# Transposing a layer norm's output by DMA, as 16-bit halves, instead of on TensorE

## The chip, the cores and the metric

The kernel runs on one core of one Trainium2 chip. The metric is the device time of one execution in microseconds (us); lower is better. The names of the engines are those of the profile: PE (TensorE, matrix products; PEld are its weight loads), DVE (VectorE), ACT (ScalarE), POOL (GpSimd), SP (SyncE, which here issues nearly all DMAs; its queue is written SPq).

## The reference

All data is 32-bit float. 2048 tokens of width 512 pass through a linear-attention half and a gated half, each behind a layer norm that is modulated by a scale and a shift; six vectors of width 512 come from a small product of `c`.

```python
mod = (_silu(c) @ w_mod).reshape(c.shape[0], 6, 1, -1)
sa, ca, ga, sb, cb, gb = (mod[:, 0], mod[:, 1], mod[:, 2], mod[:, 3], mod[:, 4], mod[:, 5])
h = _layernorm(x, axis=-1) * (1 + ca) + sa
x = x + ga * _A_ref(h, A_wqkv, A_wo)          # linear attention, 32 heads of 16
h = _layernorm(x, axis=-1) * (1 + cb) + sb    # the second layer norm
x = x + gb * _B_ref(h, B_w_gate, B_w_up, B_w_down)   # ((h Wg) * (h Wu)) Wd, Wg and Wu are 512 x 1376
```

## The kernel before, in words

**Tiles.** The 2048 tokens are 4 chunks (0 to 3) of 4 token tiles of 128. Every product is done in three matmuls on operands split into a high and a low part (`split`: ACT makes the high part, DVE or POOL the low one).

**The second layer norm** of a chunk has these steps. `xhat` (L277, ACT) makes four normalized tiles `n[j]` of 128 tokens x 512. `transpose` (L284, PE) turns them into four tiles of 128 features x 512 tokens, 16 transposes of 128x128 a chunk, into banks of PSUM. `ln2_f` (L925, ACT) applies scale `cb` and shift `sb` to each of the four and writes `f`. For chunks 2 and 3, `f` goes to memory (`kept`, L930) and is loaded back later (L111, by `Left.get`).

**The gated half** works in two sides: chunks 0 and 1, then chunks 2 and 3. A side is 11 blocks, one for each 128 columns of the two weights, so block n runs from 0 to 21. A block multiplies by a Strassen-like scheme with 7 products: `times` into the four PSUM banks a, b, c, d (`abank` to `dbank`), 6 matmuls each (L1057), in the order a11, s1, s2, a12, s3, a22, s4. Between them stand copies of one bank into another on ACT (L1063, `copy`): b from a after a11, c from b after s2; then u2, g, and u3. DVE reads the banks with L1113 (which frees d), L1122 and L1083. A bank's next product waits for the copy into it. Part s2 of a block therefore waits for the copy into b, and part s3 for the copy into c.

**What stands between.** `block` calls `also(point)` after each part: at the points a11, s1, s2, a12, s3, pe, mid and s4, lists of jobs written by hand are run. `early` holds the jobs of the attention half's end and of the second layer norm of chunks 2 and 3. The point pe, between s3 and a22, holds other matmuls (`y_a`, L871, and the down products, L1146 to L1148); their results are added to `x` by DVE (L1153) at s4 in the first side. `split_down` and `scale_down` (L1280, then ACT and DVE L206 and L207) prepare down weights; `right_load`, `right_sums`, `right_split` and `right_keep` load, sum (POOL L1002), split (ACT L1013 and L1016, POOL L1020) and store (SP L1034) the weights of blocks ahead.

Each engine runs its instructions in the order in which the program issues them, and an instruction that waits holds up all behind it on its engine. SP's queue does the same with DMAs: an issue that waits holds up later issues. Each DMA of SP has one of eight semaphores in turn, and waits until the DMA eight issues earlier has landed. Tiles in SBUF come from one pool of 99 buffers; a new tile waits for the last reader of the tile that had the buffer before.

Of the kernel before, what the change touches and what calls it, by code (L numbers as in the profile page):

```python
# [7 lines left out]

F32 = mybir.dt.float32
F32R = mybir.dt.float32r  # L10
AF = mybir.ActivationFunctionType
ALU = mybir.AluOpType
AX = mybir.AxisListType

P = 128
# [7 lines left out]
def tile_adaln_block(  # L23
# [12 lines left out]
    nc = tc.nc  # L36
    ctx.enter_context(tc.manual_schedule())
    _, S, D = x.shape
    F = w_gate.shape[1]
    KD = D // P  # L40
    NJ = 4
    CH = NJ * P
# [22 lines left out]
    def f32(ap):  # L65
        return ap.bitcast(F32)
# [3 lines left out]
    def T(p, tag, shape=(P, D), dt=F32, bufs=None):  # L70
        cnt[0] += 1
        return p.tile(list(shape), dt, tag="t" if p is tiles else tag, name=f"{tag}_{cnt[0]}", bufs=bufs)

    def B(tag, shape=(P, D), dt=F32):

        return T(tiles, tag, shape, dt)
# [11 lines left out]
    nc.gpsimd.memset(ones, 1.0)  # L88
    ones_r = consts.tile([P, P], F32R, name="ones_r")
    mask = consts.tile([P, P], F32, name="mask")  # L90
# [53 lines left out]

    idle = B("w", dt=F32R)
    idle_f = B("f")
# [15 lines left out]
    def silu_a():  # L162
        nc.tensor.transpose(ct, c_k, ident[:KD, :KD])
        nc.scalar.activation(ce, ct, AF.Exp, scale=-1.0)

# [6 lines left out]
    def mod_acc(acc, raws, ks, on=None):  # L172
        for k in ks:
            if k == 0:
                if on:
                    on.activation(acc, raws[k], AF.Copy, scale=sc[:, 0:1])
                else:
# [19 lines left out]
    def mod_row(v, pair):  # L197
        ps = bank()
        over_rows(ps, pair)
        t = consts.tile([P, D], F32, name=f"row{v}")  # L200
        nc.scalar.activation(t, ps, AF.Copy)
        return t


    def split(src, h, l, low=None):
        nc.scalar.activation(h, src, AF.Copy)  # L206
        (low or nc.vector).tensor_tensor(l, src, f32(h), op=ALU.subtract)  # L207

    def split_raw(raw, shape=(P, D), low=None):
        h = B("w", shape, F32R)  # L210
        l = B("w", shape, F32R)
        split(raw, h[:raw.shape[0]], l[:raw.shape[0]], low)
        return h, l
# [25 lines left out]
    class Norm:  # L239
        def __init__(self, tiles):  # L240
            self.tiles = tiles
            self.mv = T(small, "mv", (P, NJ, 2), bufs=6)
            self.n = [None] * NJ
            self.ps = [None] * KD
            self.t = [None] * KD

        def stats(self, *js, of=None):
            for j in js:
                st = T(small, "st", (P, 6), bufs=4)
                nc.vector.bn_stats(st, self.tiles[j] if of is None else of)  # L250
                nc.vector.bn_aggr(self.mv[:, j], st)
# [18 lines left out]
        def xhat(self, *js, on=None):  # L270
            for j in js:
                self.n[j] = B("n")
                if on:
                    on.tensor_scalar(self.n[j], self.tiles[j], self.rstd[:, j:j + 1], self.nmr[:, j:j + 1],
                                     op0=ALU.mult, op1=ALU.add)
                    continue
                nc.scalar.activation(self.n[j], self.tiles[j], AF.Identity,  # L277
                                     scale=self.rstd[:, j:j + 1], bias=self.nmr[:, j:j + 1])

        def transpose(self, *ks, of=bank):  # L280
            for k in ks:
                ps = of()
                for j in range(NJ):
                    nc.tensor.transpose(ps[:, j * P:(j + 1) * P], self.n[j][:, k * P:(k + 1) * P], ident)  # L284
                self.ps[k] = ps

        def banks(self):

            a, b, c, d = [bank() for _ in range(KD)]
            self.ps = [(a[:, :2 * P], ps_idle[:, 2 * P:]), (b,), (c,), (d,)]  # L290
# [6 lines left out]
        def modulated(self, scale, shift, *ks, keep=None, cast=None):  # L297
            for k in ks:
                h = B("h", dt=F32R)
                l = B("h", dt=F32R)  # L300
                f = B("f")
                nc.scalar.activation(f, self.ps[k], AF.Identity, scale=scale[:, k:k + 1], bias=shift[:, k:k + 1])
                if cast:
# [119 lines left out]
    halves = {}  # L423
# [222 lines left out]
    for i in range(4, NT):  # L646
        ch, j = divmod(i, NJ)
# [194 lines left out]
    def turn_a(i, of=bank):  # L842
        tps[i] = of()
        phi = phq.pop(i)
        for k in range(KD):
            nc.tensor.transpose(tps[i][:, k * P:(k + 1) * P], phi[:, k * P:(k + 1) * P], ident)

    def turn_h(i):
        pqs[i] = (B("xh", dt=F32R), B("xl", dt=F32R))
        nc.scalar.activation(pqs[i][0], tps[i], AF.Copy)  # L850

    def turn_l(i):
        h, l = pqs[i]
        nc.vector.tensor_tensor(l, tps.pop(i), f32(h), op=ALU.subtract)
# [8 lines left out]
    def y_a(i):  # L863
        pq = pqs.pop(i)
        fresh = i not in seeded
        if fresh:
            yps[i] = acc_bank()
        for k in range(KD):
            (ah, al), (bh, bl) = cut(pq, k * P, (k + 1) * P), wp[k]
            for n, (x, y) in enumerate(((ah, bh), (ah, bl), (al, bh))):  # L870
                nc.tensor.matmul(yps[i], x, y, start=fresh and k + n == 0,  # L871
                                 stop=k == KD - 1 and n == 2, skip_group_check=True)

    def y_b(i):
        ch, j = divmod(i, NJ)
        ps = yps.pop(i)
        if i in seeded:
            nc.scalar.activation(xts[ch][j], ps, AF.Copy)
            norm2[ch].stats(j, of=ps)
        else:  # L880
            nc.vector.tensor_tensor(xts[ch][j], xts[ch][j], ps, op=ALU.add)
            norm2[ch].stats(j)
# [30 lines left out]
    norm2 = {ch: Norm(xts[ch]) for ch in range(NCH)}  # L913
# [5 lines left out]
    def ln2_turn(ch, *ks, of=bank):  # L919
        norm2[ch].transpose(*ks, of=of)  # L920

    def ln2_f(ch, *ks):
        for k in ks:
            f = B("f")
            nc.scalar.activation(f, norm2[ch].ps[k], AF.Identity, scale=cb[:, k:k + 1], bias=sb[:, k:k + 1])  # L925
            norm2[ch].ps[k] = None
            if ch < 2:
                plain[ch, k] = f
            else:
                nc.sync.dma_start(kept[ch, k], f)  # L930
# [457 lines left out]
    def turned(i):  # L1388
        turn_a(i, of=acc_bank)
        turn_h(i)  # L1390
        turn_l(i)

    def ln2_x(ch, *js):
        norm2[ch].xhat(*js)

    def ln2_r(ch, a=0, b=NJ):
        norm2[ch].rstd_of(a, b, True)

    def ln2_m(ch, a=0, b=NJ):
        norm2[ch].nmr_of(a, b)  # L1400

    early = {
        (0, "a11"): [lambda: y_a(12)],
        (0, "s1"): [lambda: turned(13), lambda: L[0].split("a22"), lambda: ln2_r(2, 3, 4)],
        (0, "s2"): [lambda: L[1].split("a22")],
        (0, "pe"): [lambda: [L[k].split("s4") for k in range(KH)], lambda: y_a(13), lambda: y_b(12)],
# [3 lines left out]
        (1, "s2"): [lambda: ln2_x(2, 3)],  # L1410
        (1, "s3"): [lambda: den_t(15), lambda: den_c(15)],
        (1, "pe"): [lambda: y_a(14), lambda: y_b(14)],
        (1, "mid"): [lambda: ln2_turn(2, 0, 1, of=acc_bank)],
        (1, "s4"): [lambda: ln2_f(2, 0, 1)],
        (2, "s1"): [lambda: turned(15), lambda: ln2_turn(2, 2, 3, of=acc_bank)],
        (2, "s2"): [lambda: ln2_f(2, 2, 3)],
        (2, "pe"): [lambda: y_a(15), lambda: y_b(15), lambda: ln2_r(3)],
        (3, "s2"): [lambda: ln2_x(3, 0)],
        (3, "s3"): [lambda: ln2_x(3, 1)],
        (3, "mid"): [lambda: ln2_x(3, 2)],  # L1420
        (3, "s4"): [lambda: ln2_x(3, 3)],
        (4, "s1"): [lambda: ln2_turn(3, 0, 1, of=acc_bank)],
        (4, "s2"): [lambda: ln2_f(3, 0, 1)],
        (5, "s1"): [lambda: ln2_turn(3, 2, 3, of=acc_bank)],
        (5, "s2"): [lambda: ln2_f(3, 2, 3)],
    }

    before = None
# [12 lines left out]
    for n, (s, g, f) in enumerate(order):  # L1441
# [50 lines left out]
        if (s, f) in pair_of:  # L1492
            at_first = f == groups[g][0]
            p = pairs.setdefault((s, g), Pair())
# [20 lines left out]
        if was and was[:2] in paired and was[2] == groups_of[was[0]][was[1]][1]:  # L1515
            of, p = was[0], pairs[was[:2]]
# [87 lines left out]
```

## Time and profile before

| what | value |
|---|---|
| device time, median of 3 runs | 553.78 us (553.54 to 557.78) |
| span of the profiled execution (first to last instruction) | 552.4 us |
| busy share of PE, DVE, ACT, POOL | 99%, 78%, 54%, 32% |
| transposes at L284 in chunks 2 and 3 of the second layer norm | 32, of 272 ns each |
| data moved by DMA | 83.24 MB, 151 GB/s over the span |

No device time is listed for the profiled execution by itself: its span lies 1.1 us under the fastest run and 1.4 us under the median, and this rest is what lies around the span. A page gives each engine's busy time; the timeline gives starts and durations; a row with x4 merges four instructions. Matmuls overlap, so the spacing of starts, not the duration, is what one costs.

### The profile page before, as it was taken

To read this page: it belongs to the slowest core of one execution; us is meant where nothing else is said; L and a number is where in the kernel's file an instruction comes from. 1 tells how busy PE (TensorE), PEld (TensorE's weight loads), DVE (VectorE), ACT (ScalarE), POOL (GpSimd) and SP (SyncE) were. 2 spreads that over 40 slices of the span, in tenths; PEclk is the share of its full clock that TensorE was granted. 3 is DMA by queue.
4 is the path that set the end of the run, shared out by engine and by line. 5 is a ranking of instruction groups with operands and counts; after the bars stand their busy time and mean duration, and the time that the engine had idled before them with its cause. 6 is when DMAs were issued, how large, how long until landed. Compare 5 with 4: busy or idle time off the path is not lost. (4 is left out here: it accounts for less than half of the span.)

```text
span 552.4 us, 8146 instructions
## 1 busy us (share of the span) xinstructions
PE 545.8 (99%) x2775; PEld 460.1 (83%) x2775; DVE 432.2 (78%) x794; ACT 299.5 (54%) x535; POOL 176.8 (32%) x180
## 2 busy tenths in 40 slices
PE   8999999999999999999999999999999999999997
PEld 6888888888888888888888888878888888888886
DVE  6878779978998998865655767797577877879696
ACT  4876857456467876654545355463243534453540
POOL 2000000003527646353556644540002524242400
PEclk9999999999999999999999999999999999999999
DMA  8910224203230045195888634289786534342004
GB/s 256 373 57 1 76 77 152 77 0 77 78 115 2 0 154 189 39 316 180 285 286 274 222 123 163 87 312 391 231 259 218 173 131 138 129 146 86 1 0 153
DMA packets 58512, 83.24 MB, mean 151 GB/s; under 512 B 6564, under 2 KB 23720, under 8 KB 58472
## 3 DMA queue, kind: packets, MB, share of 16 engines
q1 hardware_dynamic: 56544, 81.16, 44.1%
q10 hardware_dynamic: 1928, 1.58, 0.9%
q8 instruction: 22, 0.36, 0.3%
q14 instruction: 18, 0.15, 0.1%
HBM read 53.02 MB, written 29.69 MB: 150 GB/s over the span
## 5 line engine op out<-in xcount | busy, mean ns | idle before, releaser
L1057 PE MATMUL bank<-h,w 128*128 128x512 f32 (+1 forms) x924 | 221.6, 391 | 0.2 <-POOL w L1020 0.2
L1057 PEld LDWEIGHTS bank<-h,w 128*128 128x128 f32 (+1 forms) x924 | 168.2, 186 | 36.2 <-POOL w L1020 0.6
L1063 ACT ACTIVATE bank<-bank 128x512 f32<-128x512 f32 (+2 forms) x46 | 26.2, 571 | 122.7 <-PE bank L1057 122.5
L1253 DVE TENSOR_TENSOR x<-acc,x 128x256 f32<-128x256 f32 x132 | 48.0, 414 | 13.7 <-PE acc L1226 13.1
L1226 PE MATMUL acc<-w,kh 128*128 128x256 f32 x308 | 57.1, 282 | 0.0
L1226 PEld LDWEIGHTS acc<-w,kh 128*128 128x128 f32 x308 | 50.6, 190 | 3.7
L1020 POOL TENSOR_TENSOR w<-raw,w 128x256 fp32r<-128x256 f32 (+3 forms) x22 | 24.7, 1121 | 73.7 <-ACT w L1013 64.1
L219 PE MATMUL bank<-w,h 128*128 128x512 f32 x112 | 44.1, 394 | 0.0
L221 PE MATMUL bank<-w,h 128*128 128x512 f32 x112 | 43.7, 390 | 0.0
L220 PE MATMUL bank<-w,h 128*128 128x512 f32 x112 | 43.6, 390 | 0.0
L1226 PE MATMUL acc<-w,kl 128*128 128x256 f32 x154 | 43.5, 283 | 0.0
L871 PE MATMUL acc<-w,xh 128*128 128x512 f32 x128 | 40.7, 399 | 0.0
L712 POOL TENSOR_TENSOR f<-h,zb 128x512 f32<-128x512 f32 x12 | 17.5, 1468 | 62.9 <-ACT zb L692 48.9
L262 POOL TENSOR_TENSOR rstd<-ve,half 128x4 f32<-128x4 f32 (+3 forms) x12 | 11.2, 935 | 81.4 <-DVE ve L259 68.0
L1083 DVE TENSOR_TENSOR phi<-bank,g 128x512 f32<-128x512 f32 (+1 forms) x22 | 15.1, 687 | 25.2 <-PE bank L1057 25.2
L1063 ACT ACTIVATE u<-bank 128x512 f32<-128x512 f32 (+1 forms) x44 | 26.1, 594 | 15.4 <-PE bank L1057 15.2
L1113 DVE TENSOR_TENSOR g<-bank,u 128x512 f32<-128x512 f32 (+1 forms) x22 | 15.2, 689 | 21.2 <-ACT u L1063 19.9
L1020 POOL TENSOR_TENSOR w<-t,w 128x512 fp32r<-128x512 f32 (+1 forms) x22 | 29.6, 1346 | 0.0
L1146 PE MATMUL acc<-w,kh 128*128 128x512 f32 (+1 forms) x76 | 29.6, 390 | 0.0
L1147 PE MATMUL acc<-w,kh 128*128 128x512 f32 (+1 forms) x76 | 29.6, 390 | 0.0
L1148 PE MATMUL acc<-w,kl 128*128 128x512 f32 (+1 forms) x76 | 29.6, 389 | 0.0
L277 ACT ACTIVATE n<-x,nmr,rstd 128x512 f32<-128x512 f32 x31 | 23.6, 808 | 10.9 <-DVE nmr L267 10.7
(204 smaller groups left out, 1187.0 us busy)
## 6 DMA issues: line engine op xcount, KB each, us to landing
right<-w SPq DMA_DIRECT2D x56, 256.0 KB, 3.7
w<-right SPq DMA_DIRECT2D x56, 256.0 KB, 4.3
x<-in_A_x_dram SPq DMA_DIRECT2D x22, 256.0 KB, 5.2
raw<-in_w_mod_dram SPq DMA_DIRECT2D x22, 256.0 KB, 3.7
raw<-in_B_w_down_dram SPq DMA_DIRECT2D x18, 256.0 KB, 3.0
side_s<-h SPq DMA_DIRECT2D x16, 256.0 KB, 2.6
h<-side_s SPq DMA_DIRECT2D x16, 256.0 KB, 5.3
raw<-in_A_wqkv_dram SPq DMA_DIRECT2D x12, 256.0 KB, 6.2
```

Of the source, the lines that this page charges most:

```text
L219: nc.tensor.matmul(ps, ah, bh, start=begin and i == 0, stop=False)
L220: nc.tensor.matmul(ps, ah, bl, start=False, stop=False)
L221: nc.tensor.matmul(ps, al, bh, start=False, stop=end and i == n - 1)
L871: nc.tensor.matmul(yps[i], x, y, start=fresh and k + n == 0, stop=k == KD - 1 and n == 2, skip_group_check=True)
L1020: sub = lambda out, x, y: (on or nc.gpsimd).tensor_tensor(out, x, f32(y), op=ALU.subtract)
L1057: mm = lambda x, y, **kw: nc.tensor.matmul(ps, x[:, k], y, skip_group_check=True, **kw)
L1063: nc.scalar.activation(out, x, AF.Copy)
L1146: nc.tensor.matmul(dn[j], hh[:n, a:b], dh[:n], start=i == 0, stop=False)
L1147: nc.tensor.matmul(dn[j], hh[:n, a:b], dl[:n], start=False, stop=False)
L1148: nc.tensor.matmul(dn[j], hl[:n, a:b], dh[:n], start=False, stop=i == n_of - 1)
L1226: mm = lambda x, y, **kw: nc.tensor.matmul(ps, x[:, a:b], y, skip_group_check=True, **kw)
L1253: nc.vector.tensor_tensor(xt[:, halves[at]], banks[b][m], xt[:, halves[at]], op=ALU.add)
```

## The change: what it does, and the diff

For chunks 2 and 3 the 32 transposes on PE go. Each `n[j]` is looked at as 16-bit numbers (128 x 1024). For each 128 features `k`, SP issues a DMA transpose of the 128 x 256 halves of each `n[j]` into a tile `cross[k]` (`turn`): 16 DMAs of 64 KB a chunk. Even partitions of `cross[k]` then hold low halves and odd ones high halves, so `gather` issues four more DMAs for each k, 64 partitions of 1 KB each, into a tile `halves[k]`: 16 more. `merge` is a DVE copy of 128 x 1024 16-bit elements that interleaves the two halves into a 32-bit tile `turned`, from which `ln2_f` reads.

```diff
+        def turn(self, *js):
+            if not self.crossed:
+                self.crossed = [B("cross", (P, 2, CH), U16) for _ in range(KD)]
+            for j in js:
+                bits = self.n[j].bitcast(U16)
+                for k, t in enumerate(self.crossed):
+                    nc.sync.dma_start_transpose(t[:, :, j * P:(j + 1) * P], bits[:, 2 * P * k:2 * P * (k + 1)])
+        def gather(self, *ks):
+            for k in ks:
+                t, halves = self.crossed[k], B("halves", (P, 2, CH), U16)
+                for m in range(2):
+                    for part in range(2):
+                        nc.sync.dma_start(halves[m * P // 2:(m + 1) * P // 2, part], t[part::2, m])
+                self.crossed[k] = halves
+        def merge(self, *ks, on=None):
+            for k in ks:
+                self.ps[k] = B("turned")
+                out = self.ps[k].bitcast(U16).rearrange("p (t m) -> p t m", m=2)
+                (on or nc.vector).tensor_copy(out, self.crossed[k].rearrange("p m t -> p t m"))
...
+    def ln2_cross(ch):
+        norm2[ch].turn(*range(NJ))
+        norm2[ch].gather(*range(KD))
+    def ln2_merge(ch, *ks):
+        norm2[ch].merge(*ks)
+        ln2_f(ch, *ks)
...
-        (1, "mid"): [lambda: ln2_turn(2, 0, 1, of=acc_bank)],
-        (1, "s4"): [lambda: ln2_f(2, 0, 1)],
-        (2, "s1"): [lambda: turned(15), lambda: ln2_turn(2, 2, 3, of=acc_bank)],
-        (2, "s2"): [lambda: ln2_f(2, 2, 3)],
+        (1, "mid"): [lambda: ln2_cross(2)],
+        (2, "s1"): [lambda: turned(15)],
+        (2, "s2"): [lambda: ln2_merge(2, 0, 1)],
+        (2, "s3"): [lambda: ln2_merge(2, 2, 3)],
...
-        (3, "s4"): [lambda: ln2_x(3, 3)],
-        (4, "s1"): [lambda: ln2_turn(3, 0, 1, of=acc_bank)],
-        (4, "s2"): [lambda: ln2_f(3, 0, 1)],
-        (5, "s1"): [lambda: ln2_turn(3, 2, 3, of=acc_bank)],
-        (5, "s2"): [lambda: ln2_f(3, 2, 3)],
+        (3, "s4"): [lambda: ln2_x(3, 3), lambda: ln2_cross(3)],
+        (4, "s4"): [lambda: ln2_merge(3, 0, 1)],
+        (5, "s1"): [lambda: ln2_merge(3, 2, 3)],
```

On ACT, at the turn from block 4 to block 5, the rows before are these (`bank_579` is b, `bank_578` is a, `bank_580` is c; `kh` are parts of block 4's product, `w` of down weights):

```order
L1016 ACTIVATE w_753_3195<-t_729_3081 128x512
L1063 ACTIVATE bank_579_2388<-bank_578_2387 128x512
L206 ACTIVATE kh_768_3294<-phi_764_3251 128x512
L206 ACTIVATE kh_770_3298<-phi_765_3254 128x512
L1063 ACTIVATE bank_580_2389<-bank_579_2388 128x512
L206 ACTIVATE w_774_3319<-raw_730_3087 128x512
L925 ACTIVATE f_776_3323<-acc_772_3302,col3_1268,col4_1324 128x512
L925 ACTIVATE f_777_3326<-acc_773_3307,col3_1268,col4_1324 128x512
```

And now, at the same place:

```order
L1042 ACTIVATE w_765_3247<-t_745_3149 128x512
L951 ACTIVATE f_780_3316<-turned_778_3312,col3_1268,col4_1324 128x512
L951 ACTIVATE f_781_3319<-turned_779_3314,col3_1268,col4_1324 128x512
L1089 ACTIVATE bank_579_2388<-bank_578_2387 128x512
L207 ACTIVATE kh_784_3356<-phi_776_3303 128x512
L207 ACTIVATE kh_786_3360<-phi_777_3306 128x512
L951 ACTIVATE f_790_3368<-turned_788_3364,col3_1268,col4_1324 128x512
L951 ACTIVATE f_791_3371<-turned_789_3366,col3_1268,col4_1324 128x512
L1089 ACTIVATE bank_580_2389<-bank_579_2388 128x512
```

Block 5's copy into b now stands behind two `f` of chunk 3, and its copy into c behind all four. Before, two of the four stood in block 4's s2 and two behind both copies.

On DVE at the same turn, the rows of the change are these (`x` is the down product's result, `raw` a down weight, `kl` the low parts to `kh`):

```order
L1179 TENSOR_TENSOR x_5_101<-acc_774_3277,x_5_101 128x512
L311 COPY turned_778_3312<-halves_740_3128 128x1024
L311 COPY turned_779_3314<-halves_741_3133 128x1024
L1306 TENSOR_TENSOR raw_746_3155<-raw_746_3155,row5_1417 128x512
L208 TENSOR_TENSOR kl_785_3357<-phi_776_3303,kh_784_3356 128x512
L208 TENSOR_TENSOR kl_787_3361<-phi_777_3306,kh_786_3360 128x512
L311 COPY turned_788_3364<-halves_742_3138 128x1024
L311 COPY turned_789_3366<-halves_743_3143 128x1024
L208 TENSOR_TENSOR w_793_3382<-raw_746_3155,w_792_3381 128x512
```

Two merges stand behind the four additions of L1153 (L1179 in the changed file), and two behind the low parts that need `kh` from ACT. Without the four rows named COPY it is the list of before.

On SP, the end of chunk 3's new DMAs and what follows them:

```order
L296 DMA_TRANSPOSE cross_739_3111<-n_735_3106 128x2x128
L304 DMA halves_740_3128<-cross_736_3108 64x512 x4
L304 DMA halves_741_3133<-cross_737_3109 64x512 x4
L304 DMA halves_742_3138<-cross_738_3110 64x512 x4
L304 DMA halves_743_3143<-cross_739_3111 64x512 x4
L112 DMA raw_746_3155<-in_B_w_down_dram 128x512
L112 DMA raw_747_3157<-in_B_w_down_dram 128x512
L1060 DMA right_5_0_3166<-w_718_3033 128x512
```

Before, the loads of `raw` stood directly behind the weight loads of L994, with neither transposes nor gathers ahead. The tile `turned_778` has the buffer of `w_718`, so the first merge also waits until the store in the last row has landed.

More of the change, by code (lines that the diff above doesn't have):

```diff
@@ L10 @@
 F32R = mybir.dt.float32r
+U16 = mybir.dt.uint16
 AF = mybir.ActivationFunctionType
@@ L245, in __init__ @@
             self.t = [None] * KD
+            self.crossed = None
         def stats(self, *js, of=None):
```

## The prediction

> **What bounds the kernel now.** I read the page's first part, then who waited for whom on PE, then PE's timeline where the 32 transposes stand.
>
> ```profile
> PE 545.8 (99%) x2775; PEld 460.1 (83%) x2775; DVE 432.2 (78%) x794; ACT 299.5 (54%) x535; POOL 176.8 (32%) x180
> PE acc L153 <- DVE w L148: 2.0, 1, 2.0
> PE bank L295 <- ACT n L277: 0.6, 1, 0.6
> PE bank L1057 <- POOL w L1020: 0.2, 1, 0.2
> ```
>
> PE is busy for 99% of the span, and its three waits (us in total, times, longest) come to 2.8 us, 2.6 of them at the start (L148 and L295 belong to it). So every microsecond of work taken from PE is one gained, and every wait put on PE is one lost: behind it no slack gives it back.
>
> ```profile
> 231.53 1.53 PE L1057 MATMUL bank<-h,w 128*128 128x512 f32 x6
> 232.89 1.03 PE L284 MATMUL acc<-ident,n 128*128 128x128 f32 x8
> 233.68 4.35 PE L1057 MATMUL bank<-h,w 128*128 128x512 f32 x18
> ...
> 282.27 5.61 PE L1057 MATMUL bank<-h,w 128*128 128x512 f32 x24
> 287.71 1.03 PE L284 MATMUL acc<-ident,n 128*128 128x128 f32 x8
> 288.50 4.34 PE L1057 MATMUL bank<-h,w 128*128 128x512 f32 x18
> ```
>
> These are the first and the last of four groups of 8 transposes (start us, duration us). A group costs the distance to the next start, 232.89 to 233.68 and 287.71 to 288.50: 0.79 us. **Removed from PE: 4 x 0.79 = 3.2 us.** That is the whole gain there can be, 0.6%. The 24 matmuls from 282.27 are block 4's a22 and s4 and block 5's a11 and s1, 6 each at 5.44 / 24 = 0.227 us; the 18 from 288.50 are block 5's s2, a12 and s3.
>
> **Block 5: the merges hold up ACT, and ACT holds up PE.** In the new order ACT makes two `f` of chunk 3 before block 5's copy into b. They need merges that stand on DVE behind the down additions. Before:
>
> ```profile
> 286.53 2.47 DVE L1153 TENSOR_TENSOR x<-acc,x 128x512 f32<-128x512 f32 x4
> 288.93 0.67 DVE L1280 TENSOR_TENSOR raw<-raw,row 128x512 f32<-128x512 f32 x1
> 289.53 1.28 DVE L207 TENSOR_TENSOR kl<-phi,kh 128x512 fp32r<-128x512 f32 x2
> 286.61 0.58 ACT L1063 ACTIVATE bank<-bank 128x512 f32<-128x512 f32 x1 [5.49 <-PE bank L1057]
> 287.10 1.14 ACT L206 ACTIVATE kh<-phi 128x512 fp32r<-128x512 f32 x2
> 290.16 0.58 ACT L1063 ACTIVATE bank<-bank 128x512 f32<-128x512 f32 x1 [1.92 <-PE bank L1057]
> L925 ACT ACTIVATE f<-acc,col,col 128x512 f32<-128x512 f32 x8 | 5.8, 775 | 2.0 <-PE acc L284 2.0
> ```
>
> The `f` themselves stay 8 in number and I price them as before, 0.78 us, though they now read SBUF; the PSUM banks that the transposes filled come free, for which nothing waits on PE. A merge's duration is not in this trace. Two rows of DVE bound it:
>
> ```profile
> L304 DVE CAST h<-f 128x512 fp32r<-128x512 f32 x12 | 5.1, 421 | 0.6 <-ACT f L302 0.6
> L1153 DVE TENSOR_TENSOR x<-acc,x 128x512 f32<-128x512 f32 x44 | 27.5, 678 | 0.1
> ```
>
> The fast bound is 0.42 us, a copy of as many bytes; the slow one is 1.22 us, L1153's row with twice the elements (its 4 take 2.47 us, so 0.60 from start to start and 0.53 for 512 elements; 0.68 + 0.53). A merge reads each pair of 16-bit elements 1 KB apart, unlike the plain copy, so I take 1.22, 1.13 from start to start. On the clock of before, where block 5's s2 could start at 287.71 without transposes:
>
> - merges at 288.93 and 290.06, done 291.28; second `f` (0.78) done 292.1; copy into b 292.0 to 292.6; **s2 starts at 292.65, 4.9 us late**;
> - `kh` until 293.6, its low parts until 294.4; merges 294.35 to 296.7; last `f` done 297.5; copy into c until 298.0. PE, having run s2 and a12 (2.7 us) by 295.4, **waits 2.65 us** before s3.
>
> Sum 4.9 + 2.7 = 7.6 us, less 3.2: **net +4.4**. With merges of 0.42 the same steps give 3.7 + 1.4 - 3.2 = +1.9.
>
> The stall is longer than any in the trace before PE's last matmul, so I looked at the clock behind that (busy us of each engine, then the granted clock, DMA share, GB/s):
>
> ```profile
> 548.00:548.50 0.50, 0.50 (x5) 0.30 (x3) 0.25 (x1) 0.00 (x0) 0.00 (x0) 1.00 1.07 363
> 551.50:552.00 0.50, 0.00 (x0) 0.00 (x0) 0.00 (x0) 0.00 (x0) 0.00 (x0) 0.81 0.00 0
> 552.00:552.40 0.40, 0.00 (x0) 0.00 (x0) 0.00 (x0) 0.00 (x0) 0.00 (x0) 0.50 0.00 0
> ```
>
> The clock falls to half some 3.2 us after PE's end at 548.5. A stall of 4.9 us can thus leave PE at half speed. Then s2 and a12 take 5.4 us and end at 298.1, just when the copy into c is done: the second wait covers it. I put 0, with 1.5 us as the upper bound (half speed for one product more, 6 x 0.227 = 1.4). The Trainium skill, TensorE: Matmul & The Clock Gate, "Part 1: The HAM clock gate", has it that one idle window of about 3.4 us halves the clock and that about 3.4 us of work restores it. The trace's end agrees with the first; by the page the sum would stay within that bound.
>
> **Block 2: the merges of chunk 2 are covered.**
>
> ```profile
> 241.92 0.69 DVE L207 TENSOR_TENSOR w<-raw,w 128x512 fp32r<-128x512 f32 x1 [1.32 <-ACT w L206]
> 244.72 0.69 DVE L1113 TENSOR_TENSOR g<-bank,u 128x512 f32<-128x512 f32 x1 [2.10 <-ACT u L1063]
> 243.29 0.62 PE L871 MATMUL acc<-w,xh 128*128 128x512 f32 x2
> 251.45 9.68 PE L1057 MATMUL bank<-h,w 128*128 128x512 f32 x42
> ```
>
> DVE merges at 242.5 to 244.9, ACT's `f` end at 245.7, u2, g and u3 at 247.2, L1113 at 247.9, the other merges at 250.2. PE runs `y_a` and down products from 243.29 to 251.45 and needs none of it before. Cost 0, with 4 us to spare.
>
> **The queue of SP: how late are the merges' inputs?** Each chunk adds 16 transposes and 16 gathers to SP. The plain issues there take 0.32 to 0.6 us:
>
> ```profile
> 224.55 0.46 SPq L994 DMA_DIRECT2D raw<-in_B_w_up_dram  x1
> 267.00 0.47 SPq L994 DMA_DIRECT2D raw<-in_B_w_up_dram  x1
> 267.51 0.94 SPq L111 DMA_DIRECT2D raw<-in_B_w_down_dram  x2
> L930 SPq DMA_DIRECT2D kept<-f x8: 319/320/339, 234.3 to 292.6; - x8
> kept<-f SPq DMA_DIRECT2D x8, 256.0 KB, 2.1
> right<-w SPq DMA_DIRECT2D x56, 256.0 KB, 3.7
> ```
>
> A gather I count as 0.45 us. For a transpose, t, no row exists. Below stands the shortest plain issue, 0.32 us. Above, the DMA engines' own time: the built program cuts a transpose into 16 pieces of 16 tokens by 128 halves.
>
> ```profile
> q1 hardware_dynamic: 56544, 81.16, 44.1%
> ```
>
> That is 0.441 x 552.4 x 16 / 56544 = 69 ns a packet. With one packet for each 256 bytes read, 256 on 16 engines, t is 1.1 us; with one for each 32 bytes written it would be 8.8. I take **t = 0.8**, between the plain issue (0.45) and the nearer packet count (1.1).
>
> Chunk 3 starts at 267.5 - 1.6 = 265.9 (two groups of transposes are gone by then). The first merge waits for the store of `right` behind the gathers and two loads: 265.9 + 16 t + 0.3 (the last landing, 2.1 us, less what issues meanwhile) + 16 x 0.45 + 2 x 0.45 + 3.7 = 278.0 + 16 t. DVE is there at 288.93 - 2.4 = 286.55. Up to t = 0.53 nothing is late. At 0.8 the store has landed at 290.8, 4.3 us late, and the whole chain of block 5 moves with it. Chunk 2 starts at 225.0: at t = 0.8 its first tile is gathered and landed at 237.8 + 1.8 + 2.1 = 241.7, where DVE comes at 242.5 - 1.6; the 4 us cover it. Behind all this stand the down weights, stores and loads of later blocks; the loads of `kept` come 5 to 10 us later, but PE then runs block 5's down products, so I put 0, up to 2 us if DVE comes late to block 6.
>
> **Sum against the profiled execution:** 552.4 - 3.2 + 7.6 + 4.3 = 561.1 of span; with the 1.4 us by which the median exceeds the span, 562.5, or 553.8 + 8.7. That is 1.6% slower.
>
> **Rivals.**
>
> - *A: transposes issue like plain DMAs* (t up to 0.6). Only ACT's hold in block 5 is left: +1.9 to +5.5, that is 555.7 to 559.3, not measurably slower. For it: the issue rows of 0.46; against it: 16 pieces each to describe. It decides at t = 0.6, where the lateness is 278.0 + 9.6 - 286.55 = 1.1 us. The Trainium skill, Advanced Engine Details and Errata, "X-Bar Transpose (TRN2)", says that such DMAs are as fast as regular ones; that would be this case, 558.2. No run here shows it yet.
> - *C: the DMA engines or the crossbar limit* (t over 1.2). Then chunk 2 is late too. At t = 1.6 its first two tiles land at 254.8 and 256.6, u3 comes at 260.1 where PE wants it at 249.85, and with the weights split behind it PE loses 12.5 us; chunk 3 is late by 278.0 + 25.6 - 286.55 = 17; with the 4.4, 34 us: 588. At t = 2.2 (a packet each to read and to write 256 bytes) 22.4 + 26.7 + 4.4 gives 607. For it: many small pieces; against it: SP's DMAs of 256 KB land in 2.1 us. The Trainium skill, VectorE: DVE Perf Modes, "The three transpose paths", gives 1309 ns for one 128x128 block of 16 bits; two to a DMA would be 2.6 us by that page, an estimate of about 620, and it advises TensorE.
> - *D: the hold costs nothing*, as if DVE merged before its additions: only the 3.2 us are left, 550.6. Against it: the order on both engines and PE's lack of slack.
>
> **Chances.** Forecast (t of 0.6 to 1.2, 559.3 to 574) 0.42; A 0.26; C 0.27; D 0.05. At t = 1.1 the forecast's sum is 4.4 + 9.1 + 4 of chunk 2 = 17.5, 571. The range runs from the fast merge of A, 555.5, to C at t = 1.6, 588: it leaves out D and the farther half of C, among it the 8.8 us bound. About 1% is what a measurement of this kernel can tell from no change. Faster by over 1% is out of reach of 3.2 us: 0.01. Within 1% are A and D: 0.30. Slower: 0.69.
>
> **What would show it.** PE's timeline should have a gap before block 5's s2 and a shorter one before its s3, each put down to ACT's copy from bank to bank; ACT's `f` from `turned` should wait for DVE's merge. The issue rows of the transposes give t, the row of the merge its 1.22 us. In block 2 PE should not wait. I am wrong if PE waits nowhere near block 5, if the gaps are in block 2, if DVE waits there for a DMA for much longer than 4 us, or if the granted clock stays low after the gap.

## Result and profile after

The changed kernel takes 592.57 us (median of 6 runs, 590.88 to 596.51) beside 554.07 us for the kernel before on the same chip: 1.0699 times as long, 95% interval 1.0671 to 1.0726, or 38.5 us more. The prediction was 562.5 us with a range of 555.5 to 588: the sign was right, the time lies above the range. The profiled execution took 590.88 us, its span is 589.1 us (552.4 before).

The page's first part and its clock row, for the kernel after:

```profile
PE 550.1 (93%) x2743; PEld 460.9 (78%) x2743; DVE 438.4 (74%) x802; ACT 301.3 (51%) x535; POOL 174.6 (30%) x180
PEclk9999999999999999969975989999999999999999
```

PE has 32 instructions fewer, yet is busy 4.3 us longer, and idle for 589.1 - 550.1 = 39.0 us against 6.6 before: 32.4 + 4.3 = 36.7, the whole difference of the spans. So two questions are left: who made PE wait, and why its work got slower. The waits on PE (us in total, times, longest):

```profile
PE bank L1083 <- ACT bank L1089: 14.8, 2, 13.4
PE acc L1172 <- DVE x L907: 11.1, 1, 11.1
PE bank L1083 <- POOL w L1046: 5.0, 1, 5.0
PE bank L1083 <- ACT kh L207: 2.3, 1, 2.3
```

These four rows, 33.2 us, name four places, and each names the engine that let PE go, not the cause. Following each back, all four end in the same queue. SP's timeline (start us, duration us, from the span's start):

```profile
225.32 21.13 SPq L296 DMA_TRANSPOSE cross<-n  x16
246.56 10.21 SPq L304 DMA_DIRECT2D halves<-cross  x16
256.89 0.99 SPq L112 DMA_DIRECT2D raw<-in_B_w_down_dram  x2
...
280.27 20.52 SPq L296 DMA_TRANSPOSE cross<-n  x16
300.89 10.14 SPq L304 DMA_DIRECT2D halves<-cross  x16
311.13 1.00 SPq L112 DMA_DIRECT2D raw<-in_B_w_down_dram  x2
312.18 4.76 SPq L1060 DMA_DIRECT2D right<-w  x7
```

For each chunk SP does nothing for 31 us but issue the new DMAs, and what stands behind them waits. The groups of the new instructions (ns min/median/max, first and last start; then form and count):

```profile
L296 SPq DMA_TRANSPOSE cross<-n x32: 1173/1243/1765, 225.3 to 299.5; - x32
L304 SPq DMA_DIRECT2D halves<-cross x32: 535/594/688, 246.6 to 310.4; - x32
L311 DVE COPY turned<-halves x8: 683/690/695, 250.5 to 322.4; 128x1024 uint16<-128x1024 uint16 x8
```

A transpose holds SP for 1.24 us, a gather for 0.59; a merge takes 0.69 us.

**Block 2.** Two rows of DVE's timeline and one of PE's (in brackets the idle time before, and what ended it):

```profile
250.46 0.69 DVE L311 COPY turned<-halves 128x1024 uint16<-128x1024 uint16 x1 [8.82 <-DMA halves<-cross]
258.97 0.68 DVE L907 TENSOR_TENSOR x<-x,acc 128x512 f32<-128x512 f32 x1
259.70 0.80 PE L1172 MATMUL acc<-w,kh 128*128 128x512 f32 x1 [11.10 <-DVE x L907]
```

The first merge waits 8.8 us for its gathers. Behind the merges on DVE stands the addition L907 of `y_b(15)`, which frees a PSUM bank of `acc`; a down product (L1172) needs that bank. PE stops at 248.6 and goes on at 259.7.

**Blocks 4 and 5.**

```profile
302.02 1.26 POOL L1046 TENSOR_TENSOR w<-t,w 128x512 fp32r<-128x512 f32 x1 [10.46 <-DMA cross<-n]
303.34 2.08 PE L1083 MATMUL bank<-h,w 128*128 128x512 f32 x4 [4.96 <-POOL w L1046]
315.56 1.30 DVE L311 COPY turned<-halves 128x1024 uint16<-128x1024 uint16 x2 [15.13 <-DMA right<-w]
316.72 1.52 ACT L951 ACTIVATE f<-turned,col,col 128x512 f32<-128x512 f32 x2 [19.15 <-DMA right<-w]
318.77 4.43 PE L1083 MATMUL bank<-h,w 128*128 128x512 f32 x12 [13.36 <-ACT bank L1089]
```

The low part of a weight on POOL takes the buffer of an `n[j]`, and that is free only when the last transposes have landed: 10.5 us for POOL, 5.0 for PE. The first merge of chunk 3 waits 15.1 us for the store of `right` whose buffer it takes, issued at 312.18 behind SP's block. ACT's first `f` starts 0.5 us after that merge has ended (315.56 + 0.69 = 316.25), let go last by another such store; the copy into b stands behind the `f`, and PE waits 13.4 us for the copy. Its other wait on ACT, 1.4 us, is for the copy into c, behind the last two `f`. A further 2.3 us come at 338, where block 6 waits for parts that stand behind late loads of `kept`.

**The slower work.** Windows of PE's first instructions after the first three gaps (length, busy us of PE, PEld, DVE, ACT and POOL, then the granted clock, DMA share, GB/s), and the row behind the gap of 2.3 us:

```profile
259.70:262.00 2.30, 2.30 (x5) 1.83 (x6) 1.35 (x4) 1.21 (x4) 0.74 (x1) 0.50 1.04 401
303.30:306.00 2.70, 2.08 (x4) 1.16 (x4) 0.00 (x0) 0.00 (x0) 1.04 (x1) 0.50 0.31 105
318.70:322.00 3.30, 3.23 (x8) 2.62 (x9) 1.38 (x3) 1.17 (x3) 0.00 (x0) 0.53 1.01 344
338.12 7.10 PE L1083 MATMUL bank<-h,w 128*128 128x512 f32 x23 [2.29 <-ACT kh L207]
```

Behind these gaps PE runs at half clock for a while; a matmul then costs 0.43 us from start to start in place of 0.227. Behind the gap of 2.3 us too the granted clock is 0.50, from 339 to 342, and 23 matmuls take 7.1 us where 24 took 5.61 before.

### The profile page after: what moved, and what is told of

Its sections match the earlier page's. It is cut to its first block, busy times and chain, and to the rows that moved or that the text cites. A ratio compares the mean times of both kernels' runs of the same rounds, so it can differ in the third digit from the quotient of the medians.

```text
span 589.1 us, 8198 instructions
## 1 busy us (share of the span) xinstructions
PE 550.1 (93%) x2743; PEld 460.9 (78%) x2743; DVE 438.4 (74%) x802; ACT 301.3 (51%) x535; POOL 174.6 (30%) x180
## 4 chain that ended last, share of the span: by engine, by line
PE 87%; SPq 7%; DMA 3%; ACT 1%; issue 1%; DVE 1%; POOL 0%; DVEq 0%; ACTq 0%; POOLq 0%
PE bank L1083 33%; PE acc L1252 9%; PE acc L897 7%; PE bank L220 5%; PE bank L222 4%; PE bank L221 4%; SPq L296 3%; SPq L304 3%; PE acc L1172 3%; PE acc L1173 3%; PE acc L1174 3%; PE acc L398 2%; PE acc L400 2%; PE acc L399 2%; PE acc L485 1%; PE bank L286 1%
## 5 line engine op out<-in xcount | busy, mean ns | idle before, releaser
L1083 PE MATMUL bank<-h,w 128*128 128x512 f32 (+1 forms) x924 | 225.9, 397 | 22.3 <-ACT bank L1089 14.8
L1083 PEld LDWEIGHTS bank<-h,w 128*128 128x128 f32 (+1 forms) x924 | 171.0, 189 | 61.3 <-ACT bank L1089 15.9
L1172 PE MATMUL acc<-w,kh 128*128 128x512 f32 (+1 forms) x76 | 30.5, 401 | 11.1 <-DVE x L907 11.1
L1109 DVE TENSOR_TENSOR phi<-bank,g 128x512 f32<-128x512 f32 (+1 forms) x22 | 15.1, 687 | 25.7 <-PE bank L1083 25.7
L1046 POOL TENSOR_TENSOR w<-t,w 128x512 fp32r<-128x512 f32 (+1 forms) x22 | 30.1, 1369 | 13.3 <-DMA cross<-n 10.5
L1173 PE MATMUL acc<-w,kh 128*128 128x512 f32 (+1 forms) x76 | 30.3, 399 | 0.0
L1252 PEld LDWEIGHTS acc<-w,kl 128*128 128x128 f32 x154 | 29.3, 191 | 0.0
```

The source lines that it names most:

```text
L1046: sub = lambda out, x, y: (on or nc.gpsimd).tensor_tensor(out, x, f32(y), op=ALU.subtract)
L1083: mm = lambda x, y, **kw: nc.tensor.matmul(ps, x[:, k], y, skip_group_check=True, **kw)
L1172: nc.tensor.matmul(dn[j], hh[:n, a:b], dh[:n], start=i == 0, stop=False)
L1173: nc.tensor.matmul(dn[j], hh[:n, a:b], dl[:n], start=False, stop=False)
L1252: mm = lambda x, y, **kw: nc.tensor.matmul(ps, x[:, a:b], y, skip_group_check=True, **kw)
```

## Experiments

In the expectations, S is the theory that each new DMA costs SP's queue a fixed time, whatever it moves, and that everything behind it in the queue comes late. Its rivals are named there; L in the first ones is that the transfers, their way through the DMA engines and their landing, set the time. The kernels e1, e4, e5 and e6 keep the change's instructions on the engines, but the normalized tiles of chunks 2 and 3 hold ones.

### e1_merge_only: the merges without the DMAs

```diff
-                (on or nc.vector).tensor_copy(out, self.crossed[k].rearrange("p m t -> p t m"))
+                (on or nc.vector).tensor_copy(out, self.n[k].bitcast(U16).rearrange("p (m t) -> p t m", m=2))
...
-        norm2[ch].turn(*range(NJ))
-        norm2[ch].gather(*range(KD))
```

> No DMA transposes and no gathers; the eight DVE merges and ACT's work behind them stay at their places (the merges copy the normalized tiles themselves, which are set to ones in chunks 2 and 3, so the output is not the reference's). Theory S (SP's issue block of 31 us a chunk is the cause): only ACT's hold in block 5 is left, with merges of 0.69 us one PE gap of 4.0 us before s2 and one of 1.8 us before s3, less 3.2 us: +2.6, about 556.7. Rival M (merges and the hold themselves cost most): over 570, with PE gaps in block 2 as well.

557.00 us, 1.0067 times the kernel before (1.0051 to 1.0084): 3.2 us more. PE's longest wait:

```profile
PE bank L1083 <- ACT bank L1089: 4.0, 2, 3.9
```

So the copies, the `f` and their places cost 3.2 us net, and the wait is the predicted one on ACT's copy before block 5's s2. The second wait is 0.2 us where 1.8 were expected, and in block 2 PE does not wait at all. The other 35 us hang on the DMAs.

### e3_half and e6_whole: the same bytes in more and in fewer transposes

In `e3_half` each transpose is issued as two of 128 halves. In `e6_whole` one transpose takes a whole `n[j]`, 4 a chunk in place of 16, and there are no gathers; `e4_no_gather` below is its counterpart.

```diff
-                    nc.sync.dma_start_transpose(t[:, :, j * P:(j + 1) * P], bits[:, 2 * P * k:2 * P * (k + 1)])
+                    for m in range(2):          # e3_half
+                        a = 2 * P * k + m * P
+                        nc.sync.dma_start_transpose(t[:, m, j * P:(j + 1) * P], bits[:, a:a + P])
...
+                nc.sync.dma_start_transpose(self.crossed[j].rearrange("p m (h t) -> p (m h) t", t=P), bits)   # e6_whole
```

> Each DMA transpose is issued as two of half the size: 32 a chunk, of 8 pieces (16 tokens x 128 halves) instead of 16. What is told apart is what an issue on SP costs. If it is per instruction, each stays at 1.24 us, the block grows by 20 us a chunk and the time goes to about 630. If it is per piece alone, each takes 0.62 us and the time stays at 592. If it is a plain issue of 0.45 us plus 0.05 us a piece, each takes 0.85 us, the block grows by 6 us a chunk, and the time is about 604. If the DMA engines set the pace and not SP, the landing time, 2.4 us, grows above 3 us.

> As the one without gathers, but one DMA transpose for each whole normalized tile: 4 a chunk, of 64 pieces each. Per instruction: 1.24 us each, a block of 5 us, nothing late, about 557 as with the merges alone. Per piece alone: 5 us each, 20 us, same time as with 16 of them, about 567. Plain issue plus 0.05 us a piece: 3.6 us each, 15 us, about 562.

`e3_half`: 631.6 us, 1.1408 times (1.1386 to 1.1431). `e6_whole`: 557.44 us, 1.0069 times (1.0049 to 1.0089). The issue rows of the two, e3 first:

```profile
L298 SPq DMA_TRANSPOSE cross<-n x64: 1113/1230/1806, 225.3 to 340.5; - x64
L295 SPq DMA_TRANSPOSE cross<-n x8: 1257/1273/2327, 225.4 to 270.8; - x8
```

As expected of a price per instruction, one kernel is 39 us slower than the change and the other within 4 us of the kernel before: transposes of 32, 64 and 256 KB hold SP for 1.23, 1.24 and 1.27 us. The price is per instruction, not per byte or per block of 128 x 128. With 8 transposes in all, `e6_whole` comes out where `e1_merge_only` does, which has none.

### e4_no_gather: the 32 transposes alone

```diff
     def ln2_cross(ch):
         norm2[ch].turn(*range(NJ))
-        norm2[ch].gather(*range(KD))
```

> The gathers are left out and the merges read the transposed tiles (with ones as normalized tiles, so the output is not the reference's): SP's block shrinks from 31 to 21 us a chunk. Theory S: PE's gap in block 2 falls from 11.1 to about 1.5 us, the long one of block 5 from 13.4 to about 3, the one behind POOL (5.0 us, behind the last transposes) stays; about 567. Rival L (the data's way through the DMA engines sets it, not SP's queue): one landing of 2 us is saved in each chunk, about 588.

572.36 us, 1.0336 times (1.0318 to 1.0355): 20 us faster than the change, where 2 x 10 us of SP's queue are gone. S's number was some 5 us too low, L's is far too high. Nor did S have all the gaps right: block 2's is 1.9 us, near its 1.5, but POOL's, which was to stay, is gone, and the long one is 11.3 us where 3 were expected. PE's longest wait:

```profile
PE bank L1083 <- ACT bank L1089: 11.3, 1, 11.3
```

### e7: one chunk at a time

In `e7_chunk2_only` chunk 3 is transposed on PE at its old points, in `e7_chunk3_only` chunk 2 is.

```diff
-        (3, "s4"): [lambda: ln2_x(3, 3), lambda: ln2_cross(3)],      # e7_chunk2_only
-        (4, "s4"): [lambda: ln2_merge(3, 0, 1)],
-        (5, "s1"): [lambda: ln2_merge(3, 2, 3)],
+        (3, "s4"): [lambda: ln2_x(3, 3)],
+        (4, "s1"): [lambda: ln2_turn(3, 0, 1, of=acc_bank)],
+        (4, "s2"): [lambda: ln2_f(3, 0, 1)],
+        (5, "s1"): [lambda: ln2_turn(3, 2, 3, of=acc_bank)],
+        (5, "s2"): [lambda: ln2_f(3, 2, 3)],
```

> Only chunk 2 goes by DMA; chunk 3 is transposed on TensorE as before. Theory S (each DMA transpose holds SP's queue for 1.24 us, and what stands behind comes late): the one long gap on PE in block 2 stays, 11.1 us, with some 2 us of matmuls at half clock behind it, less 1.6 us of transposes taken from PE: about +11.5, 565.4 us. Rival (the two chunks' stalls are one chain, the first causing the second): about the whole +38, or next to nothing here and all of it in the other run.

> Only chunk 3 goes by DMA; chunk 2 is transposed on TensorE as before. Theory S: the gaps of 5.0 (POOL's buffer), 13.4 (the store behind SP's block), 1.4 and 2.3 us stay, 22 in all, with some 5 us of matmuls at half clock, less 1.6 us: about +26, 580 us, and the two single runs add up to the change's +38.5 within 3 us. Rival (chunk 2's lateness pushes chunk 3's): well under +20 here.

566.95 us (1.0231 times, 1.0188 to 1.0273) and 578.12 us (1.043 times, 1.0391 to 1.0469), beside 553.66: 13.3 and 24.5 us more, together 37.8 of the change's 38.5. So the two chunks' costs add up, and neither causes the other's. PE's waits, of chunk 2 alone and then of chunk 3 alone:

```profile
PE acc L1172 <- DVE x L907: 11.4, 1, 11.4
```

```profile
PE bank L1083 <- ACT bank L1089: 14.0, 2, 13.5
PE bank L1083 <- POOL w L1046: 5.4, 1, 5.4
PE bank L1083 <- ACT kh L207: 1.8, 1, 1.8
```

They are the four waits of the change. POOL's wait comes first and has PE late already when block 5 begins, so the two are one delay: the copy into b waits for SP's store either way.

### e5_merge_moved: the merges at another place

```diff
# against e1_merge_only
-        (4, "s4"): [lambda: ln2_merge(3, 0, 1)],
-        (5, "s1"): [lambda: ln2_merge(3, 2, 3)],
+        (4, "mid"): [lambda: ln2_merge(3, 0, 1, 2, 3)],
```

> As e1_merge_only (no transposes or gathers by DMA, the merges read the normalized tiles, which hold ones in chunks 2 and 3), with chunk 3's merges and their f at block 4's mid instead of its s4 and block 5's s1. If the place in ACT's order is what the hold costs: the wait of 4.0 us on ACT's copy goes, only the 3.2 us of transposes are left, 550.6 us. Rival (the eight merges' time on DVE costs by itself): still 556 to 557.

551.93 us, 0.996 times (0.9944 to 0.9977): 5 us faster than e1, 1.7 faster than before. The hold was the place, not the copies' time. PE's page row gives what the transposes are worth there:

```profile
PE 542.7 (99%) x2743; PEld 456.7 (83%) x2743; DVE 441.9 (80%) x802; ACT 301.0 (55%) x535; POOL 178.8 (33%) x180
```

545.8 - 542.7 = 3.1 us less of PE, as predicted; the span is 2.2 us shorter. So this is about what the idea gives here if its DMAs cost nothing. The trace has something else, in DVE's timeline and POOL's:

```profile
241.22 1.29 DVE L311 COPY turned<-n 128x1024 uint16<-128x1024 uint16 x2
277.20 6.35 DVE L311 COPY turned<-n 128x1024 uint16<-128x1024 uint16 x4
277.84 1.74 POOL L1046 TENSOR_TENSOR w<-t,w 128x512 fp32r<-128x512 f32 x1
```

Two merges take 1.29 us while POOL is idle; four take 6.35, 1.6 each, while POOL adds, and POOL's addition takes 1.74, where the same takes 1.29 in the trace of before. Where the two run side by side, both are slower.

### e9 to e13: the whole computation with 8 transposes and no gathers

The halves end up mixed over the partitions since the transpose reads them interleaved. If DVE parts each `n[j]` into all low and all high halves first (`part`), one transpose a tile suffices and nothing has to be gathered.

```diff
+        def part(self, *js):
+            for j in js:
+                self.crossed[j] = B("parts", (P, 2 * D), U16)
+                nc.vector.tensor_copy(self.crossed[j].rearrange("p (m d) -> p m d", m=2),
+                                      self.n[j].bitcast(U16).rearrange("p (d m) -> p m d", m=2))
         def turn(self, *js):
+            for j in js:
+                t = B("cross", (P, 2 * KD, P), U16)
+                nc.sync.dma_start_transpose(t, self.crossed[j])
+                self.crossed[j] = t
         def merge(self, *js):
+            for j in js:
+                t = B("turned", (P, KD, P))
+                nc.vector.tensor_copy(t.bitcast(U16).rearrange("p k (t m) -> p (k t) m", m=2),
+                                      self.crossed[j].rearrange("p (m k) t -> p (k t) m", m=2))
+                self.crossed[j] = t
```

> The whole computation with few DMAs: VectorE first parts each normalized tile into low and high 16-bit halves (8 copies of 128x1024), SP issues one transpose for each tile (4 a chunk, 8 in all, 1.25 us each, 5 us of SP's queue a chunk in place of 31), no gathers, and the merges stand at blocks 2 and 4 mid, ahead of no copy that PE waits for. Theory S: all of it is covered and only the 3.2 us taken from PE show, 550.6 to 552 us. Rival (DVE's 16 copies of 0.69 us or ACT's 32 f of 128x128 hold PE up): 555 or more, with PE waiting for DVE or ACT in blocks 2 to 5.

560.27 us, 1.0106 times (1.0074 to 1.0138). SP's block is gone, but DVE's copies stand beside POOL (row of the groups: busy us, mean ns), and PE waits for DVE and ACT:

```profile
L294 DVE COPY parts<-n 128x1024 uint16<-128x1024 uint16 x8 | 10.4, 1344 | 0.0
PE bank L1082 <- DVE g L1147: 3.0, 2, 2.4
PE bank L1082 <- ACT bank L1088: 2.8, 1, 2.8
```

That is the rival: DVE's copies of 1.34 us in the mean and ACT's 32 small `f` hold PE up. `e10_pool_free` moves the copies (chunk 2: two at block 1's s2, two at block 2's s1; chunk 3: block 3's s2 and s3), merges in 16 copies of 128x256 a chunk at block 2's mid and block 4's s3, and so keeps `f` whole.

> The whole computation as in e9_parts_first (copies into halves first, one DMA transpose a tile, no gathers), with three edits: the copies that part and merge stand where POOL runs nothing (e9_parts_first had 0.69 us for such a copy alone and 1.6 to 1.8 beside POOL); the merges write one tile for each 128 features, in 16 copies of 128x256 a chunk, so that f is 8 whole ACT instructions in place of 32 small ones (6.5 us in place of 15.4); and chunk 3's normalized tiles are made one block earlier. If POOL's presence and the small f's cost e9_parts_first its 6.6 us: 551 to 553 us, with no wait of PE over 1 us in blocks 1 to 5, and copies of 0.69 us. Rival (DVE has no room for the copies at all): 556 or more, PE waiting for DVE's g or phi.

557.09 us, 1.0055 times (1.0034 to 1.0076), the rival's number. `part` now takes 0.69 us, but chunk 3's 16 small copies take 7.18 us beside POOL; `phi` stands behind them on DVE, `kh` waits for `phi`, and PE for `kh`, 1.5 us in block 5. The longer of the two waits below, 2.6 us at 304.6, comes in block 6, where DVE has waited 8.1 us for loads of `kept`:

```profile
277.00 7.18 DVE L310 COPY turned<-cross 128x256 uint16<-128x256 uint16 x16
PE bank L1082 <- ACT kh L207: 4.2, 2, 2.6
```

`e11_one_tile` merges in 4 copies a chunk into one fixed tile, for which the pool gives up four buffers.

> The whole computation as in e10_pool_free, where 16 merge copies of 128x256 a chunk took 5.5 and 7.2 us of DVE and held up the h of DVE and, through SP, the loads of kept: here the merges are 4 copies of 128x1024 a chunk into one fixed tile of 8 KB (four buffers fewer in the pool, 95), f stays 8 whole ACT instructions, and chunk 3's merges stand at block 4's mid behind that h, where e5_merge_moved had them at no cost. If these two were what e10_pool_free lost: 551 to 553 us, no wait of PE over 1 us. Rival (the pool of 95 buffers, or POOL beside the merges of chunk 3, costs as much): 555 or more.

558.48 us, 1.0081 times (1.0065 to 1.0096), again the rival's number. The waits of blocks 1 to 5 are down to 0.6 us at most, but a new one stands at 388 us, in the later down products:

```profile
PE acc L1251 <- DVE x L1178: 3.0, 1, 3.0
```

`e13_before_95` is the kernel before with only its pool changed (`NB = 99` to `NB = 95`); `e12_small_f` has all 99 buffers, merges for each 128 tokens and small `f`, chunk 3's merges at block 4's s2 and s3 and its last four `f` at block 5's s2, behind the copy into c.

> The kernel before with 95 buffers in place of 99 and nothing else changed. If four buffers are what e11_one_tile lost late: 3 to 5 us slower than before, 557 to 559 us. Rival (the buffers cost nothing, the loss came from the copies): 553.5 to 554.5 us.

> The whole computation, as e11_one_tile but with all 99 buffers: a merge for each 128 tokens and 32 small f, as in e9_parts_first, with chunk 3's merges at block 4's s2 and s3, before POOL starts, and its last four f behind block 5's copy into c. If what e11_one_tile lost late (PE waiting 3.0 us at 388 us of its span, with 95 buffers) was the four buffers: 551 to 554 us and no such wait. Rival (ACT's 32 small f, 15 us in place of 6.5, hold up the copies from bank to bank): 556 or more, with PE waiting for ACT in blocks 3 to 5.

`e13_before_95`: 560.86 us, 1.0118 times (1.0098 to 1.0138), with the same late wait:

```profile
PE acc L1226 <- DVE x L1153: 3.2, 1, 3.2
```

Four buffers of 99 are worth 6.5 us in this kernel (0.0118 of 553.57), more than I expected and more than the 4.5 (0.0081) that e11 lost: the buffers alone are enough to explain its loss. `e12_small_f`: 553.16 us, 1.0 times (0.9979 to 1.002), the same as before. Its copies and its largest wait but the one at the start:

```profile
L294 DVE COPY parts<-n x8: 676/685/689, 228.1 to 262.9; 128x1024 uint16<-128x1024 uint16 x8
L308 DVE COPY turned<-cross x8: 680/681/690, 247.8 to 277.5; 128x1024 uint16<-128x1024 uint16 x8
PE bank L1082 <- ACT kh L207: 1.6, 1, 1.6
```

So the transposes can leave PE without a loss, with a quarter of the DMA transposes, no gathers, and each copy at a place where PE does not wait for it and POOL does not slow it. There is no measurable gain: of the 3.1 us, 1.6 are lost again in a wait that ends at 301.6 us of its span, behind loads of `kept`. The only version faster than the kernel before, e5 by 0.4%, has no transposes at all.

## Why the prediction was wrong, step by step

1. **Removed from PE, 3.2 us: right.** e5 shows 3.1.
2. **The hold in block 5: the mechanism was right, the size near.** Its wait before s2, 4.9 us with merges of 1.22 and 3.7 with 0.42, is 3.9 in e1 with merges of 0.69; the second wait, 2.65 or 1.4, is 0.2. Net it costs 3.2 us in e1, between the +1.9 and +4.4 that I gave, and e5 shows that the place makes it.
3. **The queue of SP: the formula held, its two prices failed.** I took t = 0.8 and 0.45 us a gather. From start to start SP spends 20.6 / 16 = 1.29 us on a transpose and 10.2 / 16 = 0.64 on a gather. With these, 278.0 + 16 x 1.29 + 16 x (0.64 - 0.45) = 301.7, which is 15.1 us after DVE at 286.55; the trace has DVE waiting 15.13. To the tenth that is luck: SP's chain (280.27 to 315.56) and DVE's way to the merge (until 300.43) are each 0.5 us shorter than I had them, and the two errors cancel. The lateness was predicted as 4.3. The hold of 4.0 comes on top: 19.1 us, and PE's waits there, 5.0 for POOL and 14.8 for ACT, sum to 19.8.
4. **"Block 2: covered, 4 us to spare": this step fails outright.** I looked for what PE needs from ACT and L1113, and overlooked that the merges also stand ahead of L881 (L907 after), on which a down product's PSUM bank hangs. PE stopped for it after five groups of three matmuls; in the trace before, the sixth group starts here:

```profile
249.41 0.39 PE L1146 MATMUL acc<-w,kh 128*128 128x512 f32 x1
```

The merges of my own sum are done at 250.2 and L881 0.7 us later, so PE would have been 1.5 us late already. With SP's real prices the first merge came at 250.46 in the trace after (my 242.5) and PE waited 11.1 us; chunk 2 alone costs 13.3 us in e7. My case C has a loss here of 12.5, but at t = 1.6 and by another wait.

5. **The clock, 0 with 1.5 at most: mis-sized.** The same 2743 instructions keep PE busy 542.7 us in e5 and 550.1 after: 7.4 us more. The clock's rows show it behind four gaps: PE works at 0.50 for about 4.1, 2.1, 3.1 and 3.4 us, behind the gaps of 11.1, 5.0, 13.4 and 2.3 us. Half of these 12.7 us is lost, 6.3; the last 1.1 us I have not traced. I had priced one gap only and let the second wait of block 5 cover it. In e1 it did: at a granted clock of 0.52 s2 and a12 take 4.35 us, and the wait left over is 0.2. What I left out are the other gaps. The Trainium skill, TensorE: Matmul & The Clock Gate, "Part 1: The HAM clock gate", states that an idle window of some 3.4 us halves the clock. The trace agrees behind the three longer gaps; behind the one of 2.3 us it has 0.50 as well, so a shorter gap was enough here, while in e9 one of 2.8 us, before 294.8, left the clock at 1.00.
6. **POOL's wait for a buffer was not in the prediction.** The new tiles take part in the pool's rotation, and `n` is now held until SP's last transpose has landed. Its 5.0 us are inside the 19.8 of step 3. **Loads of `kept`, "up to 2": 2.3**, and the half clock behind it.

In sum, PE's gaps 11.1 + 19.8 + 2.3, the slower work's 7.4, less 3.1, make 37.5; the spans differ by 36.7, and the 0.8 between are small waits of the trace before and rounding. What put the time above the range are two steps: SP's price of a DMA (lateness 15.1 in place of 4.3), and block 2, whose 11.1 us I had at nothing.

Of the rivals, C had t nearly right (over 1.2) and the cause wrong: neither the DMA engines nor the crossbar limit. Four times the bytes in one instruction cost the same 1.27 us, and in e6 the same bytes cost nothing. My bounds of 1.1 and 8.8 us were counted in packets, and packets were not what SP's time goes by; the row that could have told it, an issue row of a DMA transpose, does not exist in the trace before. The Trainium skill, Advanced Engine Details and Errata, "X-Bar Transpose (TRN2)", has these DMAs as fast as regular ones. For the landing the trace comes near (2.4 us; 2.0 for the gathers of the same 64 KB); for the issue it does not, 1.24 us beside 0.32 to 0.6 for the plain rows, and here the issue decided. The same skill's VectorE: DVE Perf Modes, "The three transpose paths", gives 1309 ns for a 16-bit block of 128 x 128; the runs show about this per instruction, with one block, two or eight in it.

## What to carry to other kernels

Price a DMA by what it holds its queue for, times their number, before its bytes: 32 small transposes and 32 gathers held SP for 62 us, and everything behind them, stores that free buffers above all, came late. When work moves onto an engine that is busy only 78% of the time, go through what is queued behind it there until you reach each thing that PE needs, a PSUM bank included; and when new tiles enter a shared pool, ask whose next buffer they hold. And a stall of PE costs more than its length: behind each of the four here, down to the one of 2.3 us, PE worked at half clock for another 2 to 4 us.

## What the runs showed that I had not expected

- A DMA transpose within SBUF holds SP for 1.23 to 1.27 us whether it moves 32, 64 or 256 KB.
- A 16-bit copy of 128x1024 on DVE takes 0.69 us alone and about 1.6 beside POOL's additions of two tiles, which then take 1.74 in place of 1.29 us. The Trainium skill, GPSIMD Engine Reference, "8. Key points", says that the two share their SBUF interfaces and contend when a DVE instruction runs in a 2-port mode or reads two inputs from SBUF; the trace agrees in that both are slowed. These copies read one input; which mode they run in, no run here shows.
- Four pool buffers fewer of 99 cost the kernel before 1.2%.
